# Order of a fused attention and gated-MLP kernel: the MLP of a batch in one sequence, with fewer second exponentials on ScalarE

## Chip, core and metric

The kernel runs on one core of one Trainium2 chip. The metric is the device time of one execution in microseconds (us), the median of several. The core has five engines that run at the same time, each through its own instruction list in order: TensorE (PE, matrix products), VectorE (DVE), ScalarE (ACT), GpSimd (POOL) and SyncE (SP, which here only issues DMA transfers).

## What is computed

Eight batches of thresholded attention (8 heads, 576 tokens, 64 wide), then a gated MLP over each batch, whose gate mixes the tokens:

```python
scores = scale * np.matmul(q, k.transpose(0, 1, 3, 2))
thresh = np.max(scores, axis=-1, keepdims=True) - tau
scores = np.where(scores >= thresh, scores, -1000000000.0)
scores = scores - np.max(scores, axis=-1, keepdims=True)
attn = np.exp(scores)
attn = attn / (np.sum(attn, axis=-1, keepdims=True) + 1e-09)
x = attn @ v                                   # heads side by side: 576 x 512 per batch
# ... gated MLP of x:
h = np.maximum(x @ w_in, 0.0)                  # 512 -> 1024
u, v = h[..., :512], h[..., 512:]
v_n = (v - mean(v)) / np.sqrt(var(v) + 1e-06)  # over the 512 columns
v_s = einsum('ts,bsd->btd', w_spatial, v_n) + b_spatial[None, :, None]
out = (u * v_s) @ w_out
```

## The kernel before

The Python of the kernel issues all instructions in an order that is written out as lists of tokens. A token is a step, a number, and the distance in batches: `v3:1`, in the pass of batch 4, is v product 3 of batch 3. The order of the tokens is the order on every engine. One list each serves the passes of batches 0, 1, 2, and one all later passes; `LAST` follows the last pass, and then a closing part that does what is left of batch 6 and the whole MLP of batch 7.

```python
for it in range(B):
    for tok in ORDER[min(it, len(ORDER) - 1)].split():
        run_token(tok, it)
for tok in LAST.split():          # LAST = "W17:1 T31:1"
    run_token(tok, B)
```

A batch's attention is 18 tiles of 128 query rows, two heads at once (576 rows are four tiles of 128, and the remaining 64 rows of two pairs of heads are put into one tile). The steps of tile g:

```python
# S, K: scores on PE into one of two PSUM rings (fp32; 8 instructions of 64x64 tiles, and the last 64 columns)
# M (VectorE): negated row maximum
def top(g):
    nm = negm[g] = small.tile([P, 2], F32, name="negm")
    nc.vector.tensor_reduce(out=nm, in_=view(s_ring[g % 2], 0, [[960, 2], [1, S]]), axis=AX.X,
                            op=ALU.max, negate=True)
# B (VectorE): only for tiles in ON_ACT
def shift(g): ...                 # nm = nm * scale + tau, on 128 x 2
# E, F (ScalarE): one head each
def spread(g, h):
    ...
    if on_act(g):                 # below the threshold: times 1e30; above: kept
        nc.scalar.activation(out=e, in_=s, func=ACT.Prelu, bias=bias_,
                             scale=scale if steps[g][1] == 4 else 1.0, alpha=1e30)
    else:
        nc.scalar.activation(out=e, in_=s, func=ACT.Exp, bias=bias_)
# W (VectorE), for tiles not in ON_ACT
def mask(g):
    ef = e_ring[g % 3].rearrange("p h s -> p (h s)")
    nc.vector.scalar_tensor_tensor(out=numerators(g), in0=ef, scalar=ctau, in1=ef,
                                   op0=ALU.is_ge, op1=ALU.mult)
# Z (ScalarE), for tiles in ON_ACT
def exps(g):
    nc.scalar.activation(out=numerators(g), in_=e_ring[g % 3].rearrange("p h s -> p (h s)"),
                         func=ACT.Exp)
```

So a tile named in `ON_ACT` has its threshold and exponential on ScalarE (E, F, Z) and a small shift on VectorE, and any other tile has E, F on ScalarE and a mask on VectorE. Further steps: `T` turns two tiles of numerators with a DMA transpose from SP, `TR` (or `RP` on PE) the tile of remaining rows, `X`, `XR`, `XP` the attention's result; `P` and `R` multiply the turned numerators with v on PE, `p` and `r` divide on VectorE; `QA`, `QB`, `QR` turn q and k on PE, `qa`, `qb`, `qr` copy them out on ScalarE; `L` loads, `sq`, `sv`, `kd` shape on GpSimd; `C..`, `WS` prepare the weights.

```python
def turn_p(i, half):              # T: waits for the masks (or Z) of its two tiles
    dst = pts[i, half] = ptp.tile([P, 2, 9, P], BF16, name="pT")
    nc.sync.dma_start_transpose(out=dst..., in_=p_ring[2 * (i % 2) + half]...)
def turn_rest(m):                 # TR
    pts[m] = ptr_ring[m % 2]
    nc.sync.dma_start_transpose(out=pts[m], in_=pr_ring[m % 2])
```

The MLP of a batch: `v0` to `v4` (five products, then Relu on ScalarE `ev`, mean `n` on GpSimd, square `k` on ScalarE, normalization `N` on GpSimd), `u0` to `u4` (Relu on ScalarE `eu`), token products `s0` to `s4` (needing all normalized v and the turned spatial weights; `es`, the gate, is a multiplication on VectorE), outputs `o0` to `o3` (`eo`, a copy on ScalarE; the remaining 64 rows are computed with the next batch's `v4`). Each product takes one of two PSUM buffers (`ps_f`), while the scores hold the rest.

The closing part has six buffers more, and takes what the lists have left:

```python
rest = left(("v", Z - 1, 4), ("u", Z - 1, 1), ("o", Z - 2, 0), ("u", Z - 1, 2),
            ("o", Z - 2, 1), ("u", Z - 1, 3), ("o", Z - 2, 2), ("u", Z - 1, 4),
            ("o", Z - 2, 3))
gates, outs = (left(*[(t, Z - 1, j) for j in range(n)]) for t, n in (("s", 5), ("o", 4)))
if not rest:
    rest, gates, outs = gates + outs[:3], [], outs[3:]
run(*rest[:1], pv_rest(NPAIR // 2 - 1), *rest[1:3], x_pe(NPAIR - 2), *rest[3:6],
    pv(NPAIR - 1, 0), *rest[6:], pv(NPAIR - 1, 1), *gates[:2], x_pe(NPAIR - 1, True),
    *gates[2:])
rest = last_gmlp(Z)               # Z = 7, NPAIR = 32
next(rest)                        # v products of batch 7 (L736)
run(moe_u(Z, 0), moe_u(Z, 1))
next(rest)                        # their normalization
run(*[moe_u(Z, j) for j in range(2, 5)], *outs)
next(rest)                        # token products and outputs of batch 7
```

Of the kernel before, what the change touches and what calls it, by code (L numbers as in the profile page):

```python
# [13 lines left out]
PSUM = bass.MemoryType.PSUM  # L14

ORDER = [(
    "L8:0 K0:0 L9:0 S0:0 L7:0 S1:0 M0:0 K1:0 Ci2:0 QA1:0 M1:0 E0:0 F0:0 qa1:0 B1:0 W0:0 K2:0 QR1:0 F1:0 "
    "S2:0 E1:0 QB1:0 M2:0 Z1:0 K3:0 S3:0 qr1:0 T00:0 F2:0 kd1:0 sv1:0 M3:0 E2:0 qb1:0 K4:0 B3:0 S4:0 W2:0 "
    "E3:0 sq2:0 F3:0 L1:-1 M4:0 Z3:0 K5:0 Ci0:0 S5:0 sv2:0 B4:0 E4:0 QA2:0 M5:0 sv0:0 F4:0 T01:0 S6:0 "
    "E5:0 Z4:0 K6:0 M6:0 F5:0 qa2:0 K7:0 B6:0 QR2:0 W5:0 E6:0 S7:0 L0:-1 F6:0 QB2:0 L4:-1 M7:0 qr2:0 Z6:0 "  # L20
    "K8:0 kd2:0 sq3:0 S8:0 F7:0 M8:0 sv3:0 QB3:0 qb2:0 T10:0 E7:0 P01:0 Cis0:0 B8:0 W7:0 F8:0 S9:0 qb3:0 "
    "E8:0 K9:0 RP01:0 p01:0 sq0:-1 rp01:0 L5:-1 M9:0 Z8:0 QA3:0 L9:-1 K10:0 S10:0 F9:0 E9:0 P00:0 M10:0 "
    "T11:0 qa3:0 S11:0 B10:0 p00:0 E10:0 K11:0 QR3:0 RP00:0 F10:0 M11:0 qr3:0 Z10:0 S12:0 kd3:0 Ci1:0 "
    "B11:0 W9:0 E11:0 K12:0 Cb0:0 P10:0 F11:0 L3:-1 M12:0 rp00:0 S13:0 Z11:0 p10:0 T20:0 K13:0 QB0:-1 "
    "M13:0 E12:0 QA0:-1 F12:0 qb0:-1 B13:0 W12:0 S14:0 qa0:-1 E13:0 Cbs0:0 Ci3:0 XP0:0 K14:0 F13:0 P11:0 "
    "L6:-1 M14:0 xp0:0 sq1:-1 K15:0 Z13:0 S15:0 p11:0 F14:0 R0:0 M15:0 T21:0 E14:0 r0:0 S16:0 B15:0 W14:0 "
    "F15:0 K16:0 XP1:0 E15:0 Cis3:0 L7:-1 M16:0 Z15:0 S17:0 L2:-1 xp1:0 K17:0 B16:0 QR0:-1 E16:0 M17:0 "
    "P20:0 qr0:-1 F16:0 T30:0 kd0:-1 P21:0 Cis2:0 F17:0 p21:0 E17:0 Cis1:0 p20:0 Z16:0 L8:-1 XR0:0 "),
(
    "K0:0 S0:0 K1:0 M0:0 QR1:0 S1:0 qr1:0 kd1:0 E0:0 QA1:0 M1:0 RP10:1 F0:0 rp10:1 S2:0 B1:0 W17:1 F1:0 "  # L30
    "qa1:0 K2:0 M2:0 E1:0 T31:1 XP2:1 QB1:0 xp2:1 K3:0 qb1:0 S3:0 B2:0 W0:0 F2:0 E2:0 P30:1 M3:0 Z1:0 "
    "sq2:0 K4:0 Cs0:1 RP11:1 S4:0 L4:-1 rp11:1 p30:1 F3:0 QA2:0 M4:0 E3:0 QB2:0 qa2:0 S5:0 T00:0 qb2:0 "
    "B4:0 W3:0 E4:0 K5:0 R1:1 F4:0 M5:0 Z2:0 sv2:0 K6:0 QR2:0 S6:0 r1:1 E5:0 Cs1:1 M6:0 F5:0 XR1:1 P31:1 "
    "Z4:0 S7:0 sv3:0 p31:1 qr2:0 W5:0 E6:0 kd2:0 XP3:1 T01:0 K7:0 xp3:1 RP01:0 F6:0 M7:0 v0:1 sq3:0 "
    "rp01:0 K8:0 ev0:1 W6:0 S8:0 sv0:0 F7:0 L0:-1 E7:0 QA3:0 M8:0 v1:1 L3:-1 qa3:0 sv1:0 K9:0 W7:0 F8:0 "
    "S9:0 ev1:1 RP00:0 T10:0 M9:0 E8:0 v2:1 Css0:1 rp00:0 K10:0 ev2:1 W8:0 S10:0 F9:0 v3:1 E9:0 M10:0 "
    "n1:1 n2:1 L6:-1 Css2:1 k1:1 K11:0 L1:-1 QB3:0 ev3:1 W9:0 S11:0 E10:0 F10:0 P01:0 M11:0 Css3:1 qb3:0 "
# [965 lines left out]
```

## Time and profile before

| | |
|---|---|
| time, median of 3 (lowest to highest) | 461.59 us (460.67 to 461.69) |
| span of the profiled execution | 459.8 us |
| busy: PE / VectorE / ScalarE / GpSimd | 434.4 / 406.5 / 391.2 / 213.2 us |
| busy share of the same | 94% / 88% / 85% / 46% |
| DMA moved | 88.03 MB, mean 191 GB/s |
| chain that ended last, by engine | PE 58%, VectorE 23%, ScalarE 9%, issue 4%, GpSimd 3%, DMA 2% |

How it is read: the profile's page gives for each engine the time in which at least one of its instructions ran. PE's matrix products overlap, so its busy time is not a measure of full use. A row of a group reads: line of the kernel, engine, operation, output from input, shapes, count, then busy us and mean ns of one, then the idle time of the engine just before them and what ended it. The chain of waits is followed back from the last instruction: at each step to what released it, or to the instruction before it on its engine. Some records can be missing: of 60 second exponentials of the lists all 60 are there, in two groups (44 and 16).

### The profile page before, as it was taken

What the parts mean: (1) busy time and instruction counts of PE and PEld (TensorE: products, weight loads), DVE (VectorE), ACT (ScalarE), POOL (GpSimd) and SP (SyncE); (2) the same over time, 40 slices, a digit from 0 to 9 for tenths busy, and PEclk for the clock granted to TensorE, in tenths of its full rate; (3) what the DMA queues carried; (4) which work ended last, traced back from release to release, by engine and by line L of the source; (5) the groups of instructions that cost most, each with busy time, mean ns of one, the idle gap of its engine ahead of it and who ended that gap; (6) DMA issues with size and microseconds to landing.
All of it is one profiled execution on the core that took longest, in us unless ns stands there. A gap on an engine that the chain in (4) does not pass through costs nothing.

```text
span 459.8 us, 11001 instructions
## 1 busy us (share of the span) xinstructions
PE 434.4 (94%) x4203; PEld 226.8 (49%) x4203; DVE 406.5 (88%) x558; ACT 391.2 (85%) x686; POOL 213.2 (46%) x434
## 2 busy tenths in 40 slices
PE   8778899899999999999999999999999999999995
PEld 4334445454445545545455545555455544555542
DVE  3978999899998889999999999999999999998573
ACT  2889899799999998999899988998899988998251
POOL 1553217794734636353644617353544617156021
PEclk9999999999999999999999999999999999999999
DMA  7899989999699997998999997998999896977422
GB/s 222 234 212 204 223 187 220 206 186 203 157 208 200 208 212 160 223 208 212 181 196 212 190 265 153 229 207 210 196 182 218 185 231 116 224 122 137 112 104 103
DMA packets 222836, 88.03 MB, mean 191 GB/s; under 512 B 193600, under 2 KB 218304, under 8 KB 222784
## 3 DMA queue, kind: packets, MB, share of 16 engines
q1 hardware_dynamic: 222128, 86.45, 88.0%
q8 instruction: 33, 0.54, 0.5%
q0 software_dynamic: 160, 0.52, 0.3%
q10 hardware_dynamic: 496, 0.36, 0.3%
q14 instruction: 19, 0.16, 0.1%
HBM read 32.79 MB, written 9.44 MB: 92 GB/s over the span
## 4 chain that ended last, share of the span: by engine, by line
PE 58%; DVE 23%; ACT 9%; issue 4%; POOL 3%; DMA 2%; SPq 0%; POOLq 0%; DVEq 0%; ACTq 0%
PE s L652 18%; DVE negm L670 11%; DVE p L699 7%; PE f L586 5%; PE s L662 5%; PE f L361 5%; ACT e L684 4%; PE f L309 4%; PE f L556 4%; PE f L509 3%; PE f L615 3%; ACT e L687 2%; DVE xn L370 2%; PE f L356 1%; DMA pT<-p 1%
## 5 line engine op out<-in xcount | busy, mean ns | idle before, releaser
L670 DVE TENSOR_REDUCE negm<-s 128x2 f32<-128x1152 f32 x144 | 194.4, 1351 | 17.4 <-PE s L652 10.6
L652 PE MATMUL s<-qkT 64*64 64x512 f32 x1152 | 155.4, 618 | 7.2 <-ACT e L684 3.8
L699 DVE SCALAR_TENSOR_TENSOR p<-e,ctau 128x1152 bf16<-128x1152 f32 x84 | 127.4, 1518 | 2.0 <-ACT e L687 1.7
L687 ACT ACTIVATE e<-s,negm 128x576 f32<-128x576 f32 x168 | 119.8, 745 | 8.6 <-DVE negm L670 7.9
L684 ACT ACTIVATE e<-s,negm 128x576 f32<-128x576 f32 x120 | 83.1, 741 | 16.9 <-DVE r L368 9.8
L662 PE MATMUL s<-kd,qkT 128*128 128x128 f32 (+1 forms) x320 | 61.7, 296 | 4.2 <-ACT e L687 2.6
L662 PEld LDWEIGHTS s<-kd,qkT 128*128 128x128 f32 (+1 forms) x320 | 45.6, 181 | 35.2 <-issue 19.1
L333 POOL COPY kd<-qkT 64x64 f32<-64x64 f32 x62 | 20.0, 322 | 74.0 <-ACT qkT L327 72.1
L704 ACT ACTIVATE p<-e 128x1152 bf16<-128x1152 f32 x44 | 51.4, 1168 | 0.5
L652 PEld LDWEIGHTS s<-qkT 64*64 64x64 f32 x1152 | 31.4, 132 | 38.9 <-ACT e L684 11.4
L525 POOL TENSOR_SCALAR nmean<-sm 128x1 f32<-128x1 f32 (+1 forms) x35 | 17.0, 525 | 70.6 <-ACT vrel L517 70.1
L361 PE MATMUL f<-v,pT 128*128 128x65 bf16 x992 | 45.0, 194 | 0.0
L361 PEld LDWEIGHTS <-pT 128*128 128x128 bf16 x1024 | 41.9, 98 | 4.0 <-issue 1.6
L370 DVE TENSOR_TENSOR xn<-f,r 128x256 bf16<-128x256 f32 (+1 forms) x94 | 35.5, 378 | 2.9
L586 PE MATMUL f<-wsT,vn 128*128 128x512 bf16 x125 | 31.1, 379 | 0.0
L218 POOL CAST v<-vx 64x64 bf16<-64x64 f32 x64 | 29.8, 465 | 1.9
L531 ACT ACTIVATE sq<-vrel,nmean 128x512 bf16<-128x512 f32 (+1 forms) x35 | 25.2, 719 | 6.1 <-POOL nmean L525 6.1
L356 PE MATMUL f<-v,pT 128*128 128x130 bf16 x124 | 27.3, 220 | 3.0 <-ACT vrel L517 1.7
L189 POOL COPY kn<-kl 128x512 f32<-128x512 f32 x31 | 28.0, 902 | 3.4 <-DMA kl<-in_k_dram 3.4
L509 PE MATMUL f<-w_in,xT 128*128 128x512 bf16 x112 | 28.9, 380 | 0.3 <-ACT xT L449 0.2
L556 PE MATMUL f<-xT,w_in 128*128 128x512 bf16 x112 | 28.7, 380 | 0.0
L541 POOL TENSOR_SCALAR vn<-vrel,rs,nm 128x512 bf16<-128x512 f32 (+1 forms) x35 | 26.8, 767 | 3.8
(163 smaller groups left out, 622.4 us busy)
## 6 DMA issues: line engine op xcount, KB each, us to landing
vl<-in_v_dram SPq DMA_DIRECT2D x16, 512.0 KB, 4.5
kl<-in_k_dram SPq DMA_DIRECT2D x15, 512.0 KB, 4.9
ql<-in_q_dram SPq DMA_DIRECT2D x15, 512.0 KB, 4.6
out_dram<-oo SPq DMA_DIRECT2D x10, 512.0 KB, 3.7
uT<-in_moe_w_in_dram SPq DMA_DIRECT2D x3, 512.0 KB, 4.7
uT<-in_moe_w_spatial_dram SPq DMA_DIRECT2D x2, 576.0 KB, 5.0
vx<-in_v_dram SPq DMA_DIRECT2D x16, 64.0 KB, 4.8
pT<-p SPq DMA_TRANSPOSE x64, 5.6
```

The source lines that it names most:

```text
L361: nc.tensor.matmul(out=t[:, at + 65 * h:at + 65 * h + 65], lhsT=pt[:, 5 * h + j, :], rhs=vt[:, 6 * h + j, :], start=False, stop=(h == 1 an ...
L370: nc.vector.tensor_tensor(out=dst, in0=o[ps, g0:g1, 0:64], in1=r[ps, g0:g1].unsqueeze(2).broadcast_to([ps.stop - ps.start, g1 - g0, 64]), ...
L509: nc.tensor.matmul(out=t, lhsT=x_of(b, f, slice(c * P, (c + 1) * P)), rhs=w_in[:, f, 512:1024], start=(f == 0), stop=(f == 3))
L556: nc.tensor.matmul(out=t, lhsT=w_in[:, m, f * P:(f + 1) * P], rhs=x_of(b, m, slice(0, 512)), start=(m == 0), stop=(m == 3))
L586: nc.tensor.matmul(out=t, lhsT=vn[:, c, f * P:(f + 1) * P], rhs=wsT[:, c, 0:512], start=(c == 0), stop=(c == 4))
L652: nc.tensor.matmul(out=s[halves[k], 1024 * h:1024 * h + 512], lhsT=qks[n][halves[h], 0, m], rhs=qks[n][halves[h], 1, 0:512], start=True, s ...
L662: nc.tensor.matmul(out=view(s[rows], 512, [[448, 2], [1, 64]]), lhsT=qks[n][:, 0, m], rhs=kd_ring[n % 2], start=True, stop=True)
L670: nc.vector.tensor_reduce(out=nm, in_=view(s_ring[g % 2], 0, [[960, 2], [1, S]]), axis=AX.X, op=ALU.max, negate=True)
L684: nc.scalar.activation(out=e, in_=s, func=ACT.Prelu, bias=bias_, scale=scale if steps[g][1] == 4 else 1.0, alpha=1e30)
L687: nc.scalar.activation(out=e, in_=s, func=ACT.Exp, bias=bias_)
L699: nc.vector.scalar_tensor_tensor(out=numerators(g), in0=ef, scalar=ctau, in1=ef, op0=ALU.is_ge, op1=ALU.mult)
L704: nc.scalar.activation(out=numerators(g), in_=e_ring[g % 3].rearrange("p h s -> p (h s)"), func=ACT.Exp)
```

## The change

All four token lists and `ON_ACT` are new; nothing else in the kernel is changed. In the lists before, the MLP of a batch stretched over three later passes: v0 to v3 and u0 of batch b in the pass of b + 1, v4, u1 to u4 and the token products in that of b + 2 among the v and u products of the next batch, the outputs in that of b + 3. In the new lists all of v and u of batch b and the first token product stand in the pass of b + 1, and the other token products and the outputs in the first half of that of b + 2, ahead of the next batch's v. The MLP of a batch is thus done in one sequence, and at the end of the lists less of it is left for the closing part: the token products 1 to 4 and the outputs of batch 6, where there were also v4, u1 to u4 and token product 0 of batch 6 and the outputs of batch 5. The preparation of the spatial and output weights moves earlier for that (into the passes of batches 0 and 1).

The threshold and exponential of fewer tiles is given to ScalarE, and of more to VectorE's mask:

```diff
-ON_ACT = [(1, 3, 4, 6, 8, 10, 11, 13, 15, 16), (1, 2, 4, 12, 13, 15, 17), (2, 4, 8, 11, 12, 13, 15, 16), (0, 4, 8, 10, 11, 13, 15)]
+ON_ACT = [(1, 4, 6, 7, 13, 15), (2, 4, 12, 13, 16), (3, 4, 11, 13, 16), (0, 2, 4, 7, 13, 16)]
```

The last list, which serves the passes of batches 3 to 7:

```diff
-    "K0:0 QA1:0 S0:0 qa1:0 v4:2 M0:0 S1:0 ev4:2 B0:0 W17:1 L6:-1 u1:2 E0:0 n4:2 L5:-1 F0:0 K1:0 R1:1 "
-    "T31:1 M1:0 eu1:2 S2:0 Z0:0 r1:1 QB1:0 F1:0 K2:0 u2:2 qb1:0 M2:0 E1:0 o0:3 eu2:2 W1:0 k4:2 K3:0 QR1:0 "
-    "S3:0 eo0:3 F2:0 o1:3 M3:0 qr1:0 E2:0 L0:-1 kd1:0 P30:1 sq2:0 W2:0 E3:0 K4:0 S4:0 F3:0 p30:1 eo1:3 "
-    "S5:0 sv0:0 M4:0 T00:0 P31:1 N4:2 B4:0 K5:0 p31:1 E4:0 u3:2 M5:0 F4:0 QA2:0 sv1:0 eu3:2 S6:0 X1:1 "
-    "qa2:0 W3:0 E5:0 K6:0 QR2:0 o2:3 qr2:0 M6:0 sq3:0 F5:0 QB2:0 eo2:3 K7:0 kd2:0 W5:0 qb2:0 T01:0 S7:0 "
-    "F6:0 E6:0 P00:0 M7:0 Z4:0 o3:3 p00:0 K8:0 F7:0 S8:0 L1:-1 W6:0 eo3:3 TR0:0 u4:2 E7:0 M8:0 v0:1 eu4:2 "
-    "K9:0 ev0:1 QA3:0 B8:0 W7:0 F8:0 S9:0 n0:1 E8:0 T10:0 P01:0 M9:0 qa3:0 Z8:0 S10:0 p01:0 QR3:0 K10:0 "
-    "qr3:0 QB3:0 F9:0 M10:0 kd3:0 s0:2 L3:-1 sq0:-1 qb3:0 OUT1:3 E9:0 v1:1 B10:0 F10:0 W9:0 K11:0 E10:0 "
-    "S11:0 Z10:0 es0:2 T11:0 S12:0 M11:0 k0:1 s1:2 ev1:1 B11:0 F11:0 K12:0 n1:1 es1:2 sv2:0 R0:0 E11:0 "
-    "OUT3:3 M12:0 P10:0 sq1:-1 Z11:0 L4:-1 K13:0 r0:0 S13:0 N0:1 F12:0 p10:0 E12:0 v2:1 M13:0 T20:0 k1:1 "
-    "P11:0 ev2:1 S14:0 B13:0 p11:0 F13:0 n2:1 W12:0 E13:0 QA0:-1 K14:0 qa0:-1 s2:2 L2:-1 M14:0 Z13:0 "
-    "OUT4:3 K15:0 QR0:-1 es2:2 k2:1 S15:0 F14:0 N2:1 v3:1 M15:0 qr0:-1 E14:0 T21:0 s3:2 ev3:1 B15:0 W14:0 "
-    "F15:0 sv3:0 QB0:-1 E15:0 K16:0 S16:0 es3:2 qb0:-1 X0:0 S17:0 n3:1 M16:0 N1:1 k3:1 s4:2 Z15:0 TR1:0 "
-    "P20:0 es4:2 E16:0 kd0:-1 K17:0 p20:0 N3:1 u0:1 F16:0 M17:0 T30:0 P21:0 eu0:1 p21:0 F17:0 W16:0 E17:0 "
-    "L7:-1 L8:-1 L9:-1 ")]
+    "S0:0 K0:0 QA1:0 M0:0 s2:2 qa1:0 sv1:0 QB1:0 B0:0 es2:2 E0:0 K1:0 S1:0 W17:1 F0:0 sq2:0 qb1:0 S2:0 "
+    "M1:0 QR1:0 K2:0 qr1:0 s1:2 M2:0 kd1:0 F1:0 T31:1 E1:0 s3:2 es1:2 B2:0 K3:0 W1:0 F2:0 R1:1 E2:0 S3:0 "
+    "r1:1 L0:-1 Z2:0 S4:0 es3:2 L4:-1 Z0:0 M3:0 o0:2 P30:1 eo0:2 T00:0 F3:0 K4:0 p30:1 P31:1 E3:0 M4:0 "
+    "QA2:0 K5:0 qa2:0 S5:0 B4:0 p31:1 E4:0 F4:0 X1:1 QR2:0 M5:0 o1:2 qr2:0 kd2:0 K6:0 o2:2 sv0:0 W3:0 "
+    "E5:0 L5:-1 F5:0 S6:0 eo1:2 T01:0 S7:0 Z4:0 sq3:0 M6:0 s4:2 eo2:2 F6:0 K7:0 es4:2 QB2:0 M7:0 E6:0 "
+    "P00:0 qb2:0 TR0:0 S8:0 B7:0 p00:0 E7:0 o3:2 W6:0 F7:0 L1:-1 K8:0 eo3:2 v0:1 OUT1:2 M8:0 Z7:0 v1:1 "
+    "ev0:1 W5:0 K9:0 S9:0 ev1:1 n1:1 T10:0 E8:0 P01:0 n0:1 M9:0 sv2:0 F8:0 R0:0 sv3:0 k0:1 p01:0 S10:0 "
+    "F9:0 r0:0 QR3:0 E9:0 K10:0 v2:1 M10:0 L8:-1 qr3:0 k1:1 kd3:0 K11:0 L3:-1 sq0:-1 QB3:0 ev2:1 W8:0 "
+    "S11:0 F10:0 qb3:0 u1:1 M11:0 E10:0 T11:0 n2:1 N0:1 QA3:0 eu1:1 K12:0 W9:0 E11:0 S12:0 qa3:0 F11:0 "
+    "v3:1 M12:0 k2:1 L6:-1 S13:0 W10:0 OUT3:2 E12:0 N2:1 K13:0 F12:0 v4:1 M13:0 ev3:1 S14:0 ev4:1 T20:0 "
+    "B13:0 W11:0 u0:1 n3:1 F13:0 K14:0 E13:0 u3:1 M14:0 n4:1 eu0:1 N1:1 K15:0 k4:1 u2:1 L9:-1 W12:0 eu3:1 "
+    "S15:0 E14:0 eu2:1 P11:0 M15:0 F14:0 N4:1 P10:0 k3:1 T21:0 p11:0 S16:0 F15:0 p10:0 E15:0 N3:1 W14:0 "
+    "QA0:-1 K16:0 qa0:-1 QB0:-1 K17:0 qb0:-1 M16:0 QR0:-1 S17:0 OUT4:2 qr0:-1 Z13:0 L2:-1 u4:1 B16:0 "
+    "M17:0 kd0:-1 L7:-1 P20:0 sq1:-1 eu4:1 E16:0 s0:1 p20:0 F16:0 W15:0 F17:0 P21:0 E17:0 es0:1 T30:0 "
+    "Z16:0 p21:0 TR1:0 X0:0 ")]
 LAST = "W17:1 T31:1"
```

The lists of the first three passes (cut to their first lines; in the third, token products and outputs of batch 0 now stand here, `s1:2` to `o3:2`):

```diff
 # pass of batch 0
-    "L8:0 K0:0 L9:0 S0:0 L7:0 S1:0 M0:0 K1:0 Ci2:0 QA1:0 M1:0 E0:0 F0:0 qa1:0 B1:0 W0:0 K2:0 QR1:0 F1:0 "
 ...
+    "Ci0:0 K0:0 L8:0 S0:0 L7:0 S1:0 M0:0 K1:0 L9:0 QA1:0 M1:0 F0:0 E0:0 B1:0 W0:0 S2:0 F1:0 qa1:0 QR1:0 "
 ...
 # pass of batch 1: v4, u1 to u4, s0, WS3 and WS4 join
-    "K0:0 S0:0 K1:0 M0:0 QR1:0 S1:0 qr1:0 kd1:0 E0:0 QA1:0 M1:0 RP10:1 F0:0 rp10:1 S2:0 B1:0 W17:1 F1:0 "
 ...
+    "S10:0 W8:0 E9:0 n3:1 v4:1 F9:0 M10:0 L0:-1 Cos1:1 QR3:0 S11:0 qr3:0 Co2:1 ev4:1 W9:0 E10:0 WS1:1 "
 ...
 # pass of batch 2
-    "K0:0 S0:0 S1:0 M0:0 QR1:0 K1:0 qr1:0 QA1:0 E0:0 M1:0 u2:2 F0:0 qa1:0 W0:0 S2:0 eu2:2 F1:0 K2:0 QB1:0 "
 ...
+    "S0:0 S1:0 W17:1 K0:0 s1:2 sq2:0 M0:0 s2:2 es1:2 sv1:0 F0:0 K1:0 es2:2 E0:0 s3:2 M1:0 K2:0 QA1:0 "
 ...
```

## Prediction

> **What bounds the kernel now.** I read the page first (shares of busy time, then the costly groups), then the busy time of each engine in stretches cut at the first row maximum of each batch (VectorE, `top`, 18 in a batch), then the chain of waits, last the DMA queue's own timeline near the end. The groups that the change deals in:
>
> ```profile
> L670 DVE TENSOR_REDUCE negm<-s 128x2 f32<-128x1152 f32 x144 | 194.4, 1351 | 17.4 <-PE s L652 10.6
> L699 DVE SCALAR_TENSOR_TENSOR p<-e,ctau 128x1152 bf16<-128x1152 f32 x84 | 127.4, 1518 | 2.0 <-ACT e L687 1.7
> L704 ACT ACTIVATE p<-e 128x1152 bf16<-128x1152 f32 x44 | 51.4, 1168 | 0.5
> ```
>
> A tile costs VectorE 1.35 us for its maxima, and then either a mask on VectorE (1.52 us) or a second exponential on ScalarE (1.17 us) with a 0.2 us shift on VectorE. `ON_ACT` chooses. The stages (columns: stretch, its length, busy us of PE, weight loads, VectorE, ScalarE, GpSimd, clock, DMA share, GB/s):
>
> ```profile
> 10.64:57.52 46.88, 37.57 (x364) 18.26 (x357) 40.99 (x50) 40.61 (x62) 18.47 (x40) 1.00 0.94 220
> 57.52:107.82 50.30, 44.91 (x469) 24.04 (x472) 46.56 (x59) 46.22 (x82) 29.78 (x53) 1.00 0.98 197
> 107.82:160.05 52.23, 50.97 (x516) 26.69 (x510) 47.56 (x62) 49.25 (x88) 30.61 (x63) 1.00 0.90 196
> ...
> 264.63:316.79 52.16, 51.80 (x516) 27.17 (x512) 49.33 (x64) 47.56 (x85) 25.30 (x53) 1.00 0.98 205
> ...
> 417.10:428.03 10.93, 10.30 (x114) 5.87 (x112) 7.04 (x13) 8.30 (x17) 4.50 (x10) 1.00 0.80 139
> 428.03:459.80 31.77, 26.80 (x199) 13.24 (x199) 17.67 (x43) 9.30 (x17) 4.71 (x6) 0.98 0.28 102
> ```
>
> Batches 0, 1 and 2 take 46.88, 50.30 and 52.23 us, batches 3 to 6 then 52.41, 52.17, 52.16 and 52.17; from the first to the last maximum of batch 7 are 48.14, and from there to the end 42.70. In a settled batch three engines are nearly full: PE 51.8, VectorE 49.3, ScalarE 47.6 of 52.16. In the chain of waits of that batch PE runs unbroken from 292 to 314 us and shares the rest with VectorE. Adding PE's pieces as that chain gives them back to back (18 score groups at 0.94 to 1.02, 18 small ones at 0.22 to 0.30, ten weighings at 0.62, transposes about 4.6, v 4.6, u 4.1, token 5.0, output 3.5) I get about 50 us, so PE leaves some 2 us and VectorE 2.8.
>
> The end is a chain of its own:
>
> ```profile
> 421.75 6.23 DMA pT<-p
> ...
> 434.00 3.45 PE t L736 x16
> ...
> 442.46 3.45 PE t L615 x16
> ...
> 450.82 1.74 PE t L810 x8
> ```
>
> After the last maximum (417.10) PE has work up to the landing of the last transpose at 428.03, then 24.6 us without a gap up to 452.6; the last batch's v products (L736) start 16.9 us after that maximum.
>
> **What the Trainium skill says.** "Perfetto Trace Analysis", section "Identifying the Most-Contended Engine", tells to use occupancy for Vector and Scalar but not for Tensor. The trace agrees: PE's 99% hides about 2 us, while VectorE's 49.3 is work. "SBUF — State Buffer", section "SBUF: two separate sides", says that a VectorE operation with two SBUF inputs and a GpSimd operation that reads SBUF lock each other out. The mask reads `e` twice; its times fit, 1.40 us at least and 1.86 at most:
>
> ```profile
> L699 DVE SCALAR_TENSOR_TENSOR p<-e,ctau x84: 1404/1419/1864, 13.7 to 420.3; 128x1152 bf16<-128x1152 f32 x84
> ```
>
> "DMA: Bandwidth & Descriptors", section "Anatomy of one DMA — SWDGE (gpsimd) path", says that any semaphore wait happens on the issuing sequencer before dispatch. So a transfer stands behind the wait of the one ahead of it on the same queue. Here the issue itself is long as well, 2.48 to 4.66 us for a `pT` and about 1.3 for a `ptr` or `xT`. In the kernel before this does no harm, because `xT` and `ptr` of the last batch go out ahead:
>
> ```profile
> 411.82 1.50 SPq L407 DMA_TRANSPOSE xT<-xn  x1
> 413.42 1.31 SPq L716 DMA_TRANSPOSE ptr<-pr  x1
> 416.99 7.30 SPq L710 DMA_TRANSPOSE pT<-p  x2
> ```
>
> **The change part by part.** I counted each list's instructions batch by batch, leaving out what `on_act` drops. No product is added or removed in all: 8.6 us of PE work move out of the end (v4 and u1 to u4 of batch 6, about 4.0; four outputs of batch 5, 3.5; token product 0 of batch 6, 1.1), into batch 1 (v4, u1 to u4, token product 0, two more turns of the spatial weights, 5.7) and batch 2 (four outputs less those turns, about 2.8). `ON_ACT` goes from 10, 7, 8, then 7 in a batch to 6, 5, 5, then 6: 60 tiles become 46. So VectorE gains 14 masks, 14 x 1.52 = 21.3 us, loses 14 shifts, 2.9, and ScalarE loses 14 x 1.17 = 16.4.
>
> Batch 0: four masks more, less four shifts, is +5.2 on VectorE, 40.99 to 46.2. It stood idle 5.9 us there (mostly waits of the maxima for scores, 4.6 and 2.3 us, the wait before the first one counted); if about 3 stay, the stage is 49.2, **+2.3**. That ScalarE falls to 36 buys nothing.
>
> Batch 1: the stretch holds two more masks, two fewer shifts and one gate (0.68): VectorE 49.9. ScalarE: minus 2.3 for second exponentials, plus 1.7 for v4, 2.2 for the u evictions, 1.4 for the weight turns: 49.2. PE 44.9 + 5.7 = 50.6. Three engines at 50 need about 52.8, **+2.5**.
>
> Batch 2: three more masks, three fewer shifts: VectorE 51.5, with 1.5 idle 53.0, **+0.8**.
>
> Batches 3 to 6: one more mask, one fewer shift: 49.3 + 1.3 = 50.6. With 1.8 idle 52.4, which is 0 for batch 3 and **+0.2** for each of three others; batch 7's stretch 45.65 + 1.3 + 1.7 = 48.6, **+0.5**.
>
> The end: what used to follow the last landing, 24.6 us of PE, loses the token products and three of four outputs of batch 6, 7.5 us. But they must find room before, and there the new order puts a wait. It ends `F16 W15 F17 P21 E17 es0 T30 Z16 p21 TR1 X0`, then `W17 T31`. T30 needs mask 15. After the last maximum VectorE does that maximum (1.35), p20 (0.6) and mask 15 (1.5): T30 is issued at +3.5 and holds the queue 2.5, TR1 is issued at +6.0 and lands some 3.7 later, at +9.7; X0 goes at +7.3, T31 at +8.6, landing near +14. The closing code calls the first token product and then `pv_rest(15)`, which reads what TR1 brings, and PE is in order. PE has P20, s0, P21 and s1 to do, 3.4 us, and then stands until +9.7: 6.3 us lost. From there R, three token products, outputs, the last weighings and their turns take about 8 us of work and 2 of waits for evictions, so the last v products start near +19.5 instead of +16.9. From them to the end were 25.8 us; three outputs fewer (2.6) and perhaps 0.4 of the normalization laid bare make 23.6. In all 43.1 against 42.7, **+0.4**.
>
> Sum: 2.3 + 2.5 + 0.8 + 0.6 + 0.5 + 0.4 = 7.1 us. The new lists differ everywhere and may remove some old waits; I take 0.7 off. 461.6 + 6.4 = 468.0.
>
> **The rivals.** First, the shorter end works: TR1 lands early, or PE has enough to do until then, and the end falls by 6 us. For it: the removal of 7.5 us from the chain after the landing is certain. Against it: the fixed place of TR1 behind T30. With the stages as above this is about 462. Second, VectorE binds every batch: at 50.6 of 52.2 any late score or late ScalarE result is paid in full, and masks slow to 1.8 us beside GpSimd. Batches at 53.5 make 474. For it: the order puts five masks in a row (8 to 12). Against it: VectorE already runs at 95% with 2.8 us idle, so such lists exist. Third, the new lists are simply better packed and the batches fall to 51 us, near PE's 50: 461 with the first batches' cost, 456 with the shorter end too. Against it: VectorE would have to run at 99%. A fourth, DMA as the bound, I hold for small: its share is 0.98, but waits on transfers are 2% of the chain, and the bytes do not change.
>
> **Range and chances.** The three uncertain terms are five settled batches (each -0.7 to +1.3), the first three (4 to 8 in all) and the end (-6 to +3). Together 460 to 476. Two per cent are 452.4 and 470.8. To be faster needs second-best stages and the shorter end at once: 0.03. To be slower needs about 2.8 us above my middle, which half a microsecond in each batch gives: 0.32.
>
> **What would show it.** Right: 98 masks of 1.5 us and 46 second exponentials; VectorE near 50.6 in a settled batch; batches 0 and 1 longer by 2 us each; in the end PE waiting 5 to 7 us at `pv_rest` for `ptr`. Wrong: a settled batch under 51.5 or over 53.3, batch 0 no longer than before, or the last v products within 17 us of the last maximum.

## The result and the profile after

The changed kernel takes 466.73 us (median of 6 runs, 466.07 to 468.26) against 461.64 us (6 runs, 460.67 to 462.64): ratio 1.0116, 95% interval 1.0091 to 1.0142. It is 5.1 us slower, inside the predicted range and 1.3 us below the predicted 468.0. The mechanism named for the end was there to be seen. Three terms of the sum were off and partly made up for each other: the first batches lost 2.2 us less than predicted, the settled ones 0.7 less, the end 0.9 more.

The costly groups of the page after, the ones shown of before (masks now at L701, maxima at L672, second exponentials at L706):

```profile
L672 DVE TENSOR_REDUCE negm<-s 128x2 f32<-128x1152 f32 x144 | 194.3, 1352 | 15.9 <-PE s L654 10.4
L701 DVE SCALAR_TENSOR_TENSOR p<-e,ctau 128x1152 bf16<-128x1152 f32 x98 | 141.1, 1440 | 0.2
L706 ACT ACTIVATE p<-e 128x1152 bf16<-128x1152 f32 x30 | 34.6, 1168 | 0.3
```

98 masks, 14 more, as counted. But all masks together cost 13.7 us more, not 21.3: their mean went from 1518 to 1440 ns. The stretches of the changed kernel, again cut at first maxima (last three: from the last maximum to the landing that PE waits for, to the last batch's v products, to the end):

```profile
9.37:57.05 47.68, 37.59 (x368) 18.49 (x360) 44.11 (x50) 37.40 (x58) 27.61 (x47) 1.00 1.00 234
57.05:111.04 53.99, 51.57 (x524) 26.86 (x521) 50.57 (x61) 49.31 (x90) 34.61 (x64) 1.00 0.91 199
111.04:163.46 52.42, 51.46 (x512) 26.92 (x511) 49.67 (x63) 46.16 (x85) 27.12 (x55) 1.00 0.95 181
...
320.60:372.92 52.32, 51.87 (x515) 26.91 (x513) 49.61 (x64) 46.84 (x84) 27.51 (x53) 1.00 1.01 204
...
420.88:430.51 9.63, 2.93 (x28) 1.32 (x26) 6.22 (x10) 3.69 (x5) 0.07 (x1) 0.94 0.58 108
430.51:441.86 11.35, 10.68 (x106) 6.29 (x107) 4.38 (x11) 1.76 (x3) 0.00 (x0) 0.75 0.67 119
441.86:464.90 23.04, 18.33 (x125) 8.39 (x122) 13.19 (x34) 8.14 (x15) 4.71 (x6) 0.97 0.23 77
```

Three sums tell where the 5.1 us lie. Up to the first maximum of batch 3: 163.46 against 160.05 us, +3.4. From there to the last maximum: 257.42 against 257.05, +0.4. From there to the end: 44.02 against 42.70, +1.3. So the settled batches are nearly the same in spite of the shift of work; most of the loss lies in the first batches, into which work was moved; and the end, for which the work was moved, got longer. All three sums vary from profile to profile, as is said further down.

The end in the DMA queue's timeline of the changed kernel, and in PE's:

```profile
424.16 2.82 SPq L712 DMA_TRANSPOSE pT<-p  x1
427.08 1.32 SPq L718 DMA_TRANSPOSE ptr<-pr  x1
428.45 1.40 SPq L409 DMA_TRANSPOSE xT<-xn  x1
430.01 2.78 SPq L712 DMA_TRANSPOSE pT<-p  x1
```

```profile
423.54 1.24 PE L588 MATMUL t<-wsT,vn 128*128 128x512 bf16 x5
430.55 0.29 PE L358 MATMUL f<-v,ptr 128*128 128x130 bf16 x1 [5.78 <-DMA ptr<-pr]
430.64 0.64 PE L363 MATMUL f<-v,ptr 128*128 128x65 bf16 x8
...
431.64 2.33 PE L588 MATMUL f<-wsT,vn 128*128 128x512 bf16 x5
```

Measured from the last maximum at 420.88: T30 is issued at +3.3 (predicted +3.5), TR1 at +6.2 (+6.0), PE goes on at +9.7 (+9.7) after standing 5.78 us (6.3). Five token products took 1.24 us before the wait and 2.33 after it. The granted clock of the 11.35 us that follow is 0.75, and of the first 5.45 of them it is 0.50:

```profile
430.55:436.00 5.45, 5.45 (x30) 2.70 (x31) 1.45 (x4) 0.00 (x0) 0.00 (x0) 0.50 1.09 136
```

### The profile page after: what moved, and what is told of

Read it like the earlier page. It is cut to its first block, busy times and chain, and to the rows that moved or that the text cites. A ratio compares the mean times of both kernels' runs of the same rounds, so it can differ in the third digit from the quotient of the medians.

```text
span 464.9 us, 10978 instructions
## 1 busy us (share of the span) xinstructions
PE 434.9 (94%) x4203; PEld 225.0 (48%) x4203; DVE 415.8 (89%) x556; ACT 379.2 (82%) x674; POOL 230.2 (50%) x434
## 3 DMA queue, kind: packets, MB, share of 16 engines
HBM read 32.79 MB, written 9.44 MB: 91 GB/s over the span
## 4 chain that ended last, share of the span: by engine, by line
PE 62%; DVE 22%; ACT 7%; issue 5%; POOL 2%; DMA 1%; SPq 0%; POOLq 0%; DVEq 0%; ACTq 0%
PE s L654 20%; DVE negm L672 11%; DVE p L701 7%; PE s L664 6%; PE f L363 5%; PE f L558 5%; PE f L617 5%; PE f L588 4%; PE f L511 4%; PE f L311 3%; ACT e L689 2%; DVE xn L372 2%; PE f L358 2%; ACT e L686 2%; PE f L496 1%
## 5 line engine op out<-in xcount | busy, mean ns | idle before, releaser
L672 DVE TENSOR_REDUCE negm<-s 128x2 f32<-128x1152 f32 x144 | 194.3, 1352 | 15.9 <-PE s L654 10.4
L701 DVE SCALAR_TENSOR_TENSOR p<-e,ctau 128x1152 bf16<-128x1152 f32 x98 | 141.1, 1440 | 0.2
L335 POOL COPY kd<-qkT 64x64 f32<-64x64 f32 x62 | 14.4, 232 | 94.9 <-ACT qkT L329 93.2
L654 PEld LDWEIGHTS s<-qkT 64*64 64x64 f32 x1152 | 31.1, 131 | 40.2 <-ACT e L689 15.3
L543 POOL TENSOR_SCALAR vn<-vrel,rs,nm 128x512 bf16<-128x512 f32 (+1 forms) x35 | 34.9, 998 | 3.8
L527 POOL TENSOR_SCALAR nmean<-sm 128x1 f32<-128x1 f32 (+1 forms) x35 | 15.1, 447 | 40.2 <-ACT vrel L519 40.1
L706 ACT ACTIVATE p<-e 128x1152 bf16<-128x1152 f32 x30 | 34.6, 1168 | 0.3
L214 POOL CAST v<-vl 128x512 bf16<-128x512 f32 x32 | 26.3, 821 | 15.1 <-issue 5.5
L588 PE MATMUL f<-wsT,vn 128*128 128x512 bf16 x130 | 32.4, 388 | 0.4 <-DVE gT L602 0.4
L558 PE MATMUL f<-xT,w_in 128*128 128x512 bf16 x120 | 30.6, 380 | 0.0
L191 POOL COPY qn<-ql 128x512 f32<-128x512 f32 x31 | 20.8, 671 | 15.7 <-DMA ql<-in_q_dram 12.2
L191 POOL COPY kn<-kl 128x512 f32<-128x512 f32 x31 | 25.4, 819 | 1.9 <-DMA kl<-in_k_dram 1.9
```

The source lines that it names most:

```text
L191: nc.gpsimd.tensor_copy(out=t, in_=ld_ring[i // 2 % 2][w][:, 2 * (i % 2):2 * (i % 2) + 2].rearrange("p h c d -> p c h d"))
L558: nc.tensor.matmul(out=t, lhsT=w_in[:, m, f * P:(f + 1) * P], rhs=x_of(b, m, slice(0, 512)), start=(m == 0), stop=(m == 3))
L588: nc.tensor.matmul(out=t, lhsT=vn[:, c, f * P:(f + 1) * P], rhs=wsT[:, c, 0:512], start=(c == 0), stop=(c == 4))
L654: nc.tensor.matmul(out=s[halves[k], 1024 * h:1024 * h + 512], lhsT=qks[n][halves[h], 0, m], rhs=qks[n][halves[h], 1, 0:512], start=True, s ...
```

## The experiments

Stage lengths are from the trace of each run; times are given as ratios to the kernel before on the same chip. Three runs leave work out, as their texts say.

**The end: TR1 earlier.** The list of the last pass alone:

```diff
+ORDER[3:] = [ORDER[3]] * 4 + [ORDER[3].replace("TR1:0 ", "").replace("Z13:0 ", "Z13:0 TR1:0 ")]
```

> The changed kernel; only in the pass of batch 7 the transfer of the last remaining rows (TR1) goes out right behind tile 13's second exponential, ahead of T30. My theory (PE stands in the closing part because TR1 is issued behind T30's wait for mask 15): TR1 lands some 4 us after the last maximum, pv_rest runs without the 6 us wait, the last v products start about 15 us after the last maximum instead of 21.0, and the time falls by 5 to 7 us, to about 461. Rival (T31's landing or the products themselves set the end): within 1.5 us of 466.7.

Measured: 1.0007 (0.9990 to 1.0025), which is 1.1% or 5.0 us below the changed kernel. From last maximum to end 37.84 us instead of 44.02; the v products start 14.8 us after the maximum instead of 21.0. Its DMA queue:

```profile
420.07 1.33 SPq L719 DMA_TRANSPOSE ptr<-pr  x1
425.04 2.69 SPq L713 DMA_TRANSPOSE pT<-p  x1
427.79 2.10 SPq L410 DMA_TRANSPOSE xT<-xn  x1
430.05 2.80 SPq L713 DMA_TRANSPOSE pT<-p  x1
```

TR1 is now ahead of T30. What binds next is in the chain of waits of the same run, the landing of T31, which stands behind X0:

```profile
430.05 4.59 DMA pT<-p
434.65 0.05 issue
434.69 0.23 PE f L359
```

The rival falls. One token's place in a list cost as much as the whole change lost: 6.2 us at the end in these two traces. The loss of the first batches is still there in this run (first maximum of batch 3 at 164.09 us), but the end is now 4.9 us shorter than that of the kernel before, where the prediction's first rival had expected 6.

**The end: PE's order instead.** The lists stay, the closing part calls the remaining rows later:

```diff
-        run(*rest[:1], pv_rest(NPAIR // 2 - 1), *rest[1:3], x_pe(NPAIR - 2), *rest[3:6],
+        run(*rest[:3], x_pe(NPAIR - 2), *rest[3:6], pv_rest(NPAIR // 2 - 1),
             pv(NPAIR - 1, 0), *rest[6:], pv(NPAIR - 1, 1), *gates[:2], x_pe(NPAIR - 1, True),
```

> The changed kernel; the lists stay, and the closing part calls pv_rest after the token products, the turn of pair 30 and two outputs instead of second. Theory (the loss is PE's own order behind a late TR1, not the transfer): PE fills the wait with 6 us of products; T31, still issued at +9, lands near +14 and binds next; the v products start near +17, the time falls by 3.5 to 5.5 us, to about 462. Rival (late transfers bind whatever PE does meanwhile): under 1.5 us.

Measured: 1.0044 (1.0030 to 1.0057), 0.7% or 3.3 us below the changed kernel, a little under the expected 3.5; the end is 40.24 us. So most of the loss was PE standing in its own order, and the late queue is the rest: T31 is issued where it was, and PE waits for it instead, 1.98 us. Behind that wait the clock is 0.50 again, for 2.60 us at least:

```profile
435.47 0.23 PE L358 MATMUL f<-v,pT 128*128 128x130 bf16 x1 [1.98 <-DMA pT<-p]
```

```profile
435.80:438.40 2.60, 1.90 (x20) 1.30 (x18) 0.77 (x3) 0.37 (x1) 0.00 (x0) 0.50 0.40 154
```

**The same wait put into the kernel before.**

```diff
+ORDER[3:] = [ORDER[3]] * 4 + [ORDER[3].replace("TR1:0 ", "") + "TR1:0 "]
```

> The kernel before; only in the pass of batch 7 TR1 goes out at the end of the list, behind T30 and ahead of T31. Theory: TR1 lands at about 423 instead of before 417, PE waits about 4 us at pv_rest (natural place 419.2 us), of which the slack before T31's landing gives back about 1: 3 us slower, about 464.6. Rival (T31's landing at 428 sets the end): within 1 us of 461.6.

Measured: 1.0122 (1.0089 to 1.0156), 5.6 us slower, not 3. The end grew from 42.70 to 47.11 us, 4.4. PE's timeline of this run:

```profile
425.54 0.29 PE L357 MATMUL f<-v,ptr 128*128 128x130 bf16 x1 [3.83 <-DMA ptr<-pr]
425.62 0.64 PE L362 MATMUL f<-v,ptr 128*128 128x65 bf16 x8
...
426.63 1.47 PE L557 MATMUL f<-xT,w_in 128*128 128x512 bf16 x3
```

3.83 us of waiting, and then products at half speed: the second row of weighings (products of the turned numerators with v) starts 0.54 us after the first, 0.31 ahead of the wait, at a clock of 0.50 over the 2.46 us behind the wait and of 0.84 over the 10.5 us around it. My expectation counted the wait and not the clock. The trace of this run also has the first maximum of batch 3 2.4 us later than the first profile of the kernel before, although nothing is changed up to there; of that more below.

**One tile more on ScalarE in each settled batch of the changed kernel.**

```diff
+ORDER[3] = ORDER[3].replace("M10:0 ", "M10:0 B10:0 ").replace("W10:0 ", "Z10:0 ")
-ON_ACT = [..., (0, 2, 4, 7, 13, 16)]
+ON_ACT = [..., (0, 2, 4, 7, 10, 13, 16)]
```

> The changed kernel with one more tile (10) of batches 3 to 7 on ScalarE, 7 as before instead of 6: one mask of 1.44 us less and one shift more on VectorE, one exponential of 1.17 more on ScalarE. Theory (settled batches of 52.3 us are set by PE together with its waits, so that VectorE's load of 49.6 costs nothing): within 1.5 us of 466.7. Rival (VectorE binds the settled batches): 1.2 us a batch, 6 us faster, 460.7.

Measured: 1.0245 (1.0195 to 1.0294), slower by 1.3% against the changed kernel, which neither had expected. Batches 3 to 6 take 53.57 to 53.62 us, 1.1 to 1.3 more each, although VectorE does less. ScalarE's timeline in one of them, around the new second exponential (L707):

```profile
361.29 0.21 ACT L534 ACTIVATION_READ_ACCUMULATOR sq<-vrel,nmean 128x1 f32 x1
361.38 1.17 ACT L707 ACTIVATE p<-e 128x1152 bf16<-128x1152 f32 x1
362.44 1.38 ACT L690 ACTIVATE e<-s,negm 128x576 f32<-128x576 f32 x2
```

There is no gap: the 1.17 us stand in front of the exponentials of a later tile (L690), whose end gives a score ring back to PE. They are in the chain of waits of this batch, and PE waits 0.69 us for them:

```profile
361.50 1.05 ACT p L707
362.55 1.27 ACT e L690 x2
363.82 0.04 issue
363.86 1.09 PE s L655 x8
```

ScalarE is the least busy of the three over the batch (46.8 of 52.3 us in the changed kernel) and has nothing to spare at this spot.

**The kernel before with the new numbers of tiles, in its old order.**

```diff
+DROPS = [(3, 10, 11, 16), (1, 15), (8, 12, 15), (10,)]
+for n, drop in enumerate(DROPS):
+    for t in drop:
+        ORDER[n] = ORDER[n].replace(f" B{t}:0 ", " ").replace(f" Z{t}:0 ", f" W{t}:0 ")
+    ON_ACT[n] = tuple(t for t in ON_ACT[n] if t not in drop)
```

> The kernel before with the numbers of ScalarE tiles of the changed one: 14 tiles (3, 10, 11, 16 of batch 0; 1, 15 of batch 1; 8, 12, 15 of batch 2; 10 of the later ones) go to VectorE's mask at the place of their second exponential; the sequence of the MLP stays. It is one part of the change alone. By the reasoning of the prediction: batch 0 +2.3, 1 +1, 2 +0.8, later ones +0.2 each, in all +5 us, 467. Rival (the masks cost nothing in time, as the later batches of the changed kernel suggest; the loss is in the moved MLP and the end): within 2 us of 462.

Measured: 1.0412 (1.0351 to 1.0473), 19 us slower, far more than either. Its stretches:

```profile
9.44:62.79 53.35, 42.60 (x375) 20.65 (x368) 44.45 (x51) 37.92 (x59) 20.56 (x41) 0.90 0.85 205
...
115.16:171.20 56.04, 50.51 (x511) 26.70 (x510) 51.06 (x63) 46.29 (x85) 32.71 (x63) 1.00 0.84 175
...
278.57:332.14 53.57, 51.70 (x508) 27.16 (x512) 50.62 (x65) 46.37 (x84) 26.57 (x53) 1.00 0.96 200
```

A settled batch has VectorE at 50.6 us, just what I had predicted for the changed kernel, and it is 1.4 us longer, nearly the whole of the mask that came. Three masks in batch 2 cost 3.8 us (56.04 against 52.23 to 52.26). Batch 0, with four, takes 53.35 against 46.88 to 48.70 in three profiles with the old list, but its clock is 0.90; batch 1, with two, takes 52.37, inside the range of the old list (49.00 to 52.52). With m1 this says that in a settled batch one tile moved in either direction, in a list not made for it, cost 1.1 to 1.4 us. It isn't so at every spot: t5_tile17_on_act, below, moves a tile in batch 1 at no cost in time.

**Load taken away, one engine at a time.** The changed kernel without some masks:

```diff
 def mask(g):
+    if g in (27, 28) or (g >= 54 and g % 18 == 10):
+        return
```

> The changed kernel without two masks of batch 1 (tiles 9 and 10) and without one mask of each batch from 3 on (tile 10); these numerators are left stale. It takes 2 x 1.44 us from VectorE in batch 1 and 1.44 in each settled batch and adds nothing elsewhere. Theory: in the settled batches (52.3 us) VectorE is not what binds, the stage shortens by less than 0.5 us; in batch 1 (54.0) VectorE is one of three engines near 50, the stage shortens by 1 to 2.5. Rival (VectorE binds everywhere): 1.4 us in a settled batch.

without some second exponentials:

```diff
 def exps(g):
+    if g in (22, 30) or (g >= 54 and g % 18 == 7):
+        return
```

> The changed kernel without the second exponentials of tiles 4 and 12 in batch 1 and of tile 7 in each batch from 3 on (stale numerators): 2 x 1.17 us less on ScalarE in batch 1, 1.17 in a settled batch. Theory (one more tile on ScalarE made each settled batch 1.25 us longer, so ScalarE's place in the chain of scores, maxima and exponentials counts): a settled batch shortens by 0.4 to 1.2 us. Rival (it was only the spot of that tile, ScalarE has 5 us free): under 0.3. Batch 1: 0.5 to 2.

and with half of some products' terms (the v products, then the outputs):

```diff
-    for f in range(4):
+    for f in (range(4) if b else (0, 3)):
 ...
-    for f in range(4):
+    for f in (range(4) if b == 0 else (0, 3)):
```

> The changed kernel with half of the terms of the v products 0 to 3 of batch 0 (PE 1.7 us less, in the pass of batch 1) and of the outputs 0 to 3 of batches 1 to 7 (1.7 us less in each pass from batch 3 on); the rest of the sum is left out. Theory (PE carries the chain of a settled batch, 51.9 of 52.3 us busy, 50 of it work): a settled batch shortens by 1.0 to 1.7 us, batch 1 by 0.5 to 1.7. Rival (PE only waits for the others): under 0.5.

Lengths of the stages, first maximum to first maximum, us:

| | batch 1 | 3 | 4 | 5 | 6 |
|---|---|---|---|---|---|
| changed kernel | 53.99 | 52.32 | 52.50 | 52.32 | 52.32 |
| VectorE less: 2.9 in batch 1, 1.4 in a later one | 53.96 | 51.86 | 52.61 | 52.24 | 51.86 |
| ScalarE less: 2.3, 1.2 | 54.05 | 52.32 | 52.50 | 52.34 | 52.33 |
| PE less: 1.7, 1.7 | 54.04 | 52.06 | 52.33 | 52.06 | 52.06 |

Ratios to the kernel before: 1.0096 (1.0067 to 1.0126), 1.0107 (1.0075 to 1.0139), 1.0059 (1.0025 to 1.0093). Most of what the third gains lies in the end (41.44 us instead of 44.02), where outputs are halved too. My theory of PE (1.0 to 1.7 us a batch) falls, and so does the one of ScalarE; VectorE's (under 0.5 us) holds in the settled batches. These gains are no larger than what the same lists vary by: in the other profiles with the changed kernel's last list, batches 3 to 6 take 52.3 to 53.0 us. But 51.86 and 52.06 lie below all of those.

The chains of waits, summed by engine, say more. In batch 6 the changed kernel's chain has 44.8 us of PE and 5.9 of VectorE. With one mask less it is PE alone, 51.6 of 51.86 us. With less PE work it has 23.4 of PE, 21.3 of VectorE and 3.2 of ScalarE, and the batch takes 52.06. So in this batch two paths of nearly the same length seem to lie side by side, PE's own work and one that goes through VectorE and ScalarE, and shortening one leaves the other. Shortening both at once was not tried.

Batch 1 doesn't answer to any of the three, although VectorE and PE are both over 50 us in it. But the two masks taken there ran at 85.5 and 88.2 us, in a stretch (79.7 to 92.5) in which the chain is PE's; most of those on the chain (57 to 66 and 103 to 111 us) were left.

**A better version.** Beside the early TR1, the last mask and T31 are done inside the last pass, ahead of X0:

```diff
+ORDER[3:] = [ORDER[3]] * 4 + [ORDER[3].replace("TR1:0 ", "").replace("Z13:0 ", "Z13:0 TR1:0 ")
+                                  .replace("E17:0 es0:1 T30:0 ", "E17:0 W17:0 es0:1 T30:0 ").replace("Z16:0 p21:0 ", "Z16:0 T31:0 p21:0 ")]
```

> The changed kernel; in the pass of batch 7 alone TR1 goes out early as in t1_ptr_early, the last mask (tile 17) is done inside that pass right behind mask 15 instead of after the list, and T31 goes out behind T30 and ahead of X0. Theory: T31 is issued near +6.1 us after the last maximum instead of +8.3 and lands near +10.7 instead of +12.9; the v products start 2 us earlier than in t1_ptr_early, and the time falls 2 us below it, ratio to before 0.996. Rival (after the early TR1, PE's own work sets the start of the v products): as t1_ptr_early, 1.0007.

Measured: 0.9975 (0.9958 to 0.9993), 459.99 us (22 runs) against 461.13 (51 runs): it beats the kernel before by a quarter of a per cent, less than expected. The end is 36.88 us, 1.0 less than in t1_ptr_early. The chain of waits there goes through the two masks on VectorE and the gate behind them, and then is PE's but for one division, up to the v products:

```profile
422.63 2.74 DVE p L703 x2
425.37 0.61 DVE gT L604
425.98 0.04 issue
426.02 0.22 PE f L360
...
434.66 3.45 PE t L740 x16
```

So the rival was half right: PE no longer waits for T31. But the moved mask took something back: PE stands 1.30 us for the gate behind it, and weighs the remaining rows 5.20 us after the last maximum, 3.87 in t1_ptr_early.

Two attempts to go further changed the border of batches 1 and 2, where VectorE runs without a gap. The first moved a mask behind the first maximum of batch 2 (and mask 15 of the last pass ahead of p20):

```diff
+                                  .replace("p20:0 F16:0 W15:0 ", "W15:0 p20:0 F16:0 ")]
+ORDER[2] = ORDER[2].replace("W17:1 ", "").replace("M0:0 ", "M0:0 W17:1 ", 1)
```

> As t3_end_mended, and mask 15 ahead of p20 in the pass of batch 7, and in the pass of batch 2 the mask of tile 17 of batch 1 behind the first maximum instead of ahead of it. Theory: 0.5 us from T30's earlier issue, and 0 to 1.5 us from a first maximum of batch 2 that needn't wait for a mask: ratio 0.993 to 0.996. Rival (VectorE's queue only swaps two things): as t3_end_mended.

Measured: 1.0029 (1.0010 to 1.0048). Batch 1 became 0.3 us shorter and batch 2 1.55 longer: a mask in another place of the same queue, at its full length. The end gained nothing (36.84 us).

The second gave that tile to ScalarE, which stands idle 2.77 us there:

```diff
+ORDER[1] = ORDER[1].replace(" M17:0 ", " M17:0 B17:0 ").replace(" Z16:0 ", " Z16:0 Z17:0 ")
-ON_ACT = [..., (2, 4, 12, 13, 16), ...]
+ON_ACT = [..., (2, 4, 12, 13, 16, 17), ...]
```

> As t3_end_mended, with tile 17 of batch 1 on ScalarE as in the kernel before: the mask of 1.73 us that stands on VectorE right ahead of the first maximum of batch 2 goes, a shift of 0.2 comes, and a second exponential of 1.17 goes where ScalarE stood idle 2.77 us waiting for that maximum. Theory (at the border of batches 1 and 2 VectorE's queue is the chain, so the mask costs its full length): the stretch from the first maximum of batch 1 to that of batch 2 falls by 1.0 to 1.5 us, ratio to before 0.994 to 0.996. Rival (as with tile 10 of the later batches, more on ScalarE delays the next exponentials): 0.9975 or above.

Measured: 0.9976 (0.9958 to 0.9994), as without it; from first to first maximum 53.50 us instead of 53.74, and batch 2 then 52.94 instead of 52.44. VectorE's timeline of this run shows the maximum now waiting for PE:

```profile
109.84 0.68 DVE L605 TENSOR_TENSOR gT<-f,uT 128x512 bf16<-128x512 f32 x1
111.02 1.36 DVE L675 TENSOR_REDUCE negm<-s 128x2 f32<-128x1152 f32 x1 [0.50 <-PE s L667]
```

The theory falls: PE's scores come hardly earlier than the mask ended.

**The kernel before once more.**

> The kernel before once more, to see how far its own first stages vary: the profile above had 46.88 and 50.30 us for batches 0 and 1, b1_ptr_late, which is the same up to batch 7, had 48.70 and 52.52 with a lower granted clock. Settled batches 52.2 in both. Theory (the first batches of the kernel before leave PE gaps, in which its clock can drop, so they vary by 2 us from run to run): somewhere in that range, total 460.7 to 464.

Measured: 1.0006 (0.9979 to 1.0034). Batches 0 and 1 took 47.47 and 49.00 us in this profile, 46.88 and 50.30 in the first, 48.70 and 52.52 in b1_ptr_late, which is the same up to there; the later ones agree within 0.1. The first maximum of batch 3 thus lies at 160.05, 158.17 and 162.45 us, against 163.46 in the changed kernel. In the longest, the clock of batch 0 is 0.93:

```profile
10.00:57.00 47.00, 38.15 (x354) 18.93 (x352) 39.28 (x50) 39.98 (x61) 16.66 (x40) 0.93 0.92 219
```

## Why the prediction was right, and where its steps were off

**The end** (predicted +0.4, measured +1.3). T30, TR1 and PE's restart came within 0.3 us of the predicted times (X0 and T31, 7.6 and 9.1 us after the last maximum, were up to 0.5 late), and in their predicted order: T30 behind mask 15, TR1 behind T30, PE in order behind TR1. Undoing that one place (t1_ptr_early, -5.0 us), letting PE work around it (t2_rest_later, -3.3), and putting it into the other kernel (b1_ptr_late, +4.4 in the end) show it as cause. The term that was mis-sized is "the last v products start near +19.5": it was +21.0, of which the shorter rest of the end (23.0 us, predicted 23.6) gave 0.6 back. What I left out is PE's clock. Of the 11.35 us from PE's restart to the v products, PE is busy 10.68; at a mean clock of 0.75 that is about 8.0 us of full-speed work (an estimate from these two numbers), just the predicted "about 8 us". The slow clock added 2.7, and the waits for evictions were 0.7 instead of 2.

"TensorE: Matmul & The Clock Gate", section "Part 1: The HAM clock gate (the "warmup" mystery)", says that after an idle window of about 3.4 us PE runs at half its clock until it has been busy for as long. The traces agree on the half: behind waits of 5.78 and 3.83 us the clock is 0.50 and the same products take 1.7 to 1.9 times as long, while in t1_ptr_early the 8 us after the last maximum run at 1.00. They differ on the length: in t2_rest_later the clock fell behind a wait of 1.98 us, in t1_ptr_early it stayed behind one of 1.81, and behind the 5.78 us the half clock lasted 5.45 us of unbroken work.

**The first batches** (+5.6 predicted to the first maximum of batch 3, +3.4 measured against the first profile). Batch 0 was predicted +2.3 and took +0.8, but began 1.27 us earlier, so its end lay 0.5 us sooner (the two other profiles of the old lists begin as early, at 9.44 and 8.97 us, so the early start is not the change's). The step that failed is the load, "is +5.2 on VectorE": VectorE gained 3.1 us. The four masks cost 5.4 us (their mean fell from 1581 to 1496 ns) and the shifts took 1.5 less, not 0.8; what remains of the difference is overlap of instructions. The idle time left, 3.6 us, was near the guess of "about 3". "Batch 0 no longer than before" was named as a sign of being wrong, and it nearly came: 47.7 us lies between the 46.9 and 48.7 of the old lists' profiles. Batch 1 was predicted +2.5 and took +3.7, with engine loads that came out near the count (VectorE 50.6 for 49.9, PE 51.6 for 50.6, ScalarE 49.3 for 49.2). It is the part of the loss that stands clear of the variation: 53.7 to 54.9 us in five profiles of the new lists, 49.0 to 52.5 in three of the old. Batch 2 was predicted +0.8 and took +0.2, with 49.7 us of VectorE instead of 51.5.

How much of the +3.4 is the change is known only roughly: the three profiles of the old lists put it between +1.0 and +5.3. And what holds batch 1 at 54 us stays open: it gave nothing for less VectorE, less ScalarE or less PE in the tiles and products taken. GpSimd was not tried. It has 5.0 us of the chain of waits there, in which it shapes v and k for later tiles, after standing 5.66 us at the first mean of the MLP's v products, for ScalarE's copy; two of the three profiles of the old lists have nothing of GpSimd in the chain of batch 1, the first has 12.2 us.

**The settled batches** (+0.6 predicted for batches 3 to 6 and +0.5 for batch 7's stretch, measured +0.55 and -0.2). The four batches came out as predicted, though five more profiles whose lists are the same there put them at +0.8 to +1.5. But the sum behind it was off: VectorE has 49.6 us in a batch and not 50.6, and stands idle 2.7 and not 1.8. The size that was off is the mask: "14 x 1.52 = 21.3 us". Over one settled batch the groups read, before and after:

```profile
L699 DVE SCALAR_TENSOR_TENSOR p<-e,ctau 128x1152 bf16<-128x1152 f32 x12 | 18.5, 1541 | 0.2 <-ACT e L687 0.2
```

```profile
L701 DVE SCALAR_TENSOR_TENSOR p<-e,ctau 128x1152 bf16<-128x1152 f32 x12 | 16.9, 1411 | 0.0
```

(The first window counts one mask of the batch before it, which reaches 0.08 us into it: 11 and 12 a batch.) Eleven masks at 1541 ns are 17.0 us, twelve at 1411 are 16.9: the extra mask cost VectorE nothing, since the masks no longer wait for GpSimd. From the first maximum of batch 3 to the last maximum, 24 of 54 masks of the kernel before take 1.58 to 1.84 us, and each of the 24 overlaps an instruction of GpSimd; in the changed kernel all 59 take 1.40 to 1.43, although 45 of them overlap one. GpSimd's normalization of v in the same windows went the other way:

```profile
L541 POOL TENSOR_SCALAR vn<-vrel,rs,nm 128x512 bf16<-128x512 f32 (+1 forms) x5 | 3.8, 767 | 0.5
```

```profile
L543 POOL TENSOR_SCALAR vn<-vrel,rs,nm 128x512 bf16<-128x512 f32 (+1 forms) x5 | 5.0, 997 | 0.5
```

One of the five takes 1.91 us instead of 0.77; it starts 0.14 us behind the start of a mask:

```profile
361.36 1.40 DVE L701 SCALAR_TENSOR_TENSOR p<-e,ctau 128x1152 bf16<-128x1152 f32 x1
361.50 1.91 POOL L543 TENSOR_SCALAR vn<-vrel,rs,nm 128x512 bf16<-128x512 f32 x1
```

That fits the exclusive lock of "SBUF — State Buffer", section "SBUF: two separate sides", by which whoever comes first holds the shared ports and the other waits; I had used the page for the spread of the masks and not asked who would wait in the new order. In the old order b2_on_act_alone comes to the figure of the rival "VectorE binds every batch", 53.6 us a batch at 50.6 of VectorE. That VectorE alone binds there isn't shown: the chain of waits of such a batch has 15.3 us of VectorE and 32.4 of PE.

**The sum** was near for a partly wrong reason. The counts of instructions held; but pricing a tile by its mean duration and adding it to an engine's load says little where lists are fitted: one tile moved costs 1.1 to 1.4 us a settled batch in a list not made for it (m1, b2), and in the new list the one more mask came with 0.1 to 0.4 us a batch on average. The 0.7 us taken off for "new lists may remove some old waits" was a guess in the right direction.

## What to carry to other kernels

Work taken off the end of a kernel pays only if what remains there can start: look for the first instruction of the closing part in every engine's order, and for the transfers that stand ahead of its own in their queue. When a static order is filled to 90% on three engines, a balance of loads doesn't tell the time. The spot in the list matters as much, and a change of division can need a new order, so look at the chain of waits around a spot before moving work there. Where the trace shows it, as here behind waits of 1.98, 3.83 and 5.78 us, a wait on TensorE is to be counted with the slow products that follow it.

## What the runs showed that was not expected

- After a wait of 3.83 us, and in another run of only 1.98, PE's products ran at a clock of 0.50, and a wait of 5.78 us left a mean clock of 0.75 over the next 11 us.
- The hold-ups between VectorE's masks and GpSimd changed sides with the order: masks 1541 to 1411 ns, the normalization on GpSimd 767 to 997, in a settled batch of nearly the same length.
- Taking 1.4 us from VectorE or 1.7 from PE shortened a settled batch by 0.5 us at most: with a mask less the chain of a batch is PE's alone (51.86 us), with less PE work it runs through VectorE and ScalarE as well (52.06).
- The first two batches of the unchanged lists varied by 4.7 us in their sum (96.5 to 101.2), the settled ones by less than 0.1.
